# Half-array products strictly in turn, and a new order of the steps of the last two thirds, in a sketched-attention and multiplicative-FFN kernel

## The chip, the cores and the metric

The kernel runs on one core of a Trainium2 chip. The core has five engines with a queue of instructions each: TensorE (PE in the profile, its weight loads as PEld), VectorE (DVE), ScalarE (ACT), GpSimd (POOL) and SyncE (SP), which issues the transfers here. The metric is the device time of one execution in microseconds (us). Each engine runs its own instructions in the order in which the program lists them; engines wait for each other by semaphores.

## The reference

Inputs are float64. First comes attention with a polynomial sketch, for 4 batches, 4 heads, 1088 positions and head size 32, with sketches of 8 rows:

```python
def phi(x):
    a = np.einsum('rd,bhsd->bhsr', S1, x)
    b = np.einsum('rd,bhsd->bhsr', S2, x)
    return np.einsum('bhsi,bhsj->bhsij', a, b).reshape(*x.shape[:-1], r * r)
q_p, k_p = (phi(q), phi(k))
kv = np.einsum('bhsf,bhsd->bhfd', k_p, v)
z = np.sum(k_p, axis=2)
num = np.einsum('bhsf,bhfd->bhsd', q_p, kv)
den = np.einsum('bhsf,bhf->bhs', q_p, z)[..., None] + 1e-06
attn = num / den
```

The result, as x with 4352 rows and 128 columns, goes through a multiplicative FFN with 1024 inner columns; the output is float32:

```python
a = x @ w1
b = x @ w2
h = a * b @ w3
return h @ w_out
```

## The kernel before

**Steps and their order.** `make_steps` defines some 1,100 named steps; each one issues one or a few instructions, or transfers. The text `ORDER` lists all names once, and the last function runs the steps in this order and chains the instructions of each engine, so that ORDER fixes every engine's queue. An engine that waits holds up all that stands behind it in its own queue. Four more tables belong to ORDER: `POOL` names the steps that run on GpSimd instead of VectorE (`on(name)`), `CPV` names copies that run on VectorE instead of ScalarE (`cp(name)`), and `SLOTS` gives for each kind of tile the buffer that every new tile takes, in the order in which ORDER creates them. Kind "b" is the eight PSUM banks. A tile that takes a buffer waits until all who used its former tile are done. The transfers on SP's queue are issued in turn, and each bulk load waits until the fourth bulk transfer before it has landed.

**Weights.** `wN.load`, `.c`, `.m`, `.j`, `.a0`, `.a1` fetch a quarter or an eighth of the float64 weights into one of three buffers (kind "raw") and make float32 of them: c and m on ScalarE read the buffer and so release it, j runs on VectorE, a on GpSimd. w0 and w1 make w1 and w2, w2 makes w_out (`wo`), w3 to w10 the eight row blocks of w3. `fK.t`, `.m`, `.o` fold block K of w3 with w_out into `w3o`: a transposition on VectorE, 8 matmuls, a copy.

**Keys and queries.** The steps `kB.*` make batch B's key sketch, its sum and its product with v (`kv0` to `kv3` and `kvr`, the last for the 64 rest positions, from `vB.load` and `vB.loadr`). `kB.ab` makes the sketch of the keys and `kB.abt` turns it. The steps `qG.*` make x, transposed, for group G of tokens: `tr`, `A0`, `C0`, `C1`, `At`, `Ct`, the arithmetic of the quotient, `phi`, `pT`, then `x` (matmuls into four banks) and `xT` (copies out of them). Group "r" holds the 64 rest positions of all batches. q4 stands for groups 4 and 5, q6 for 6 and 7.

**FFN, groups 0 to 3 and r.** For each of 8 column blocks c, `gG.ca` and `gG.cb` are the products with w1 and w2, `cc` copies the first out of PSUM, `cm` multiplies. `gG.co` accumulates the product with `w3o`, `gG.oT` turns the sum on VectorE, `gG.st` stores it (four transfers). Group r has half the columns, and `gr.co0` and `gr.co1`.

**FFN, groups 4 to 7: the block part.** `seven(g)` computes the products with w1 and w2 for two groups at once with seven products instead of eight, each with 64 rows. Half a (u = 0) holds the chain for w1 and uses array rows 0 to 63, half b (u = 1) the one for w2 and rows 64 to 127, so that a product of a and one of b can run together. For each g (4 or 6), i (0 to 3) and half there are the steps `h{g}.{i}{a or b}{1..7}` (products) and c, d, e, i (copies by ScalarE) and f, g, h (adds by VectorE). In their order: 1 into bank X, copy c; 5 into bank Y, copy d; 6 onto X, copy e; 3 onto Y, add f; 7 onto X, add g; 2 into bank Z, add h; 4 onto X, which half a copies (i). Product 6 waits for copy c, 7 for e, 4 for g, and 3 for d, as the bank is read in between. Then `m11`, `m12`, `m22` multiply halves a and b out of SBUF (VectorE or GpSimd), and `m21` takes half b from the bank (VectorE). `h{g}.s1` to `s4` make the sums of inputs that the products need: 5 needs s1, 6 needs s2, 7 needs s3, 3 needs s4, and s2 reads s1, s4 reads s2. The `v.*` steps make the same for the weights. `g4.co` to `g7.co` are the products with `w3o`, `g.oS` rescales (VectorE or GpSimd).

In ORDER the block part of h4 comes after the output products of groups 0 to 3, then those of g4 and g5, then h6, then those of g6 and g7 mixed with group r. The lines that the change touches are the tables SLOTS, POOL, CPV and ORDER; the lines that the prediction names are 1644 (products of the block part), 1651 (its copies), 1656 (adds), 1678 and 1683 (m), 1519 (x), 1625 (s2), 1697 and 1707 (a and b), 1732 (o), 1721 (o of group r), 1739 (oT), 1745 (oS), 1548 (stores), 432 (weight loads), 967 (q loads), 579 (v loads), 1325 (tr), 719 (ab) and 526 (folds).

Of the kernel before, what the change touches and what calls it, by code (L numbers as in the profile page):

```python
# [43 lines left out]

WARM = [27, 2, 3, 4, 4, 4, 1, 2, 1, 1, 2, 2, 1, 1]
# [49 lines left out]
g2.7c w7.m w7.c k3.kT1 k0.Nr q4.tr g1.1m g1.0m g2.2a q3.al q3.p2 q3.p12 q3.dn q3.de g1.4b g2.4a g2.5a g2.5c w3.load
k3.rest0 w5.j w6.j w6.a0 g1.4m k3.gram0 k3.gram1 k3.gram2 k3.gram3 k3.gram4 k3.Gm k3.Gt q3.rc k3.Ga k3.kT0 q3.bs k3.Gb
g2.3a w5.a1 g2.2c w2.m q2.restT q4.max w7.j g2.1a g2.1c g2.1b g2.1m g2.5b g2.5m g2.7b g1.6b g2.6a k3.Gc g2.3c k2.Nb
q4.l2 q3.load q3.restT qr.max qr.l2 qr.l1 g2.4c w3.m g2.6c g2.0b g2.0a g2.0c w8.load w4.load v3.zero v3.loadr v2.load
v3.load v2.loadr k2.Nr q3.phi0 q3.pT0 g0.2m w7.a1 w2.a0 g1.6m kr1.kp k3.T0 w6.a1 w7.a0 w2.a1 w5.a0 k3.T1 g2.2b g2.6b
g2.4b g2.3b f6.t w3.c k3.Ta g2.7m k3.Tb g2.4m k3.Tc g2.6m f4.t w3.j w3.a1 q3.x f6.m q3.xT0 w3.a0 g3.7a q4.l1 g3.3a v.s  # L100
g3.7c f6.o f4.m f4.o g2.2m q4.A0 g2.0m g3.3c g2.3m q4.rm f3.t k3.ab k3.N0 w10.load q4.C0 q4.C1 k3.N1 k2.kp0 g3.6a
k3.abt k3.kp0 q6.tr w4.m f0.t q4.At k2.kp1 q4.Ct g3.0a f3.m w4.c g3.6c w10.c w10.j g3.7b g3.5a g3.3b f0.m g3.7m q4.sm
k3.kp1 f0.o k2.kv0 k2.kv3 k2.kv1 k2.kv2 k3.kv0 k2.kvr k3.kv1 k3.kv3 k3.kv2 v.t g3.0c k3.kvr k3.Na w4.j w4.a0 w4.a1
f2.t g3.3m q4.st q4.sh k3.Nb f1.t k2.kvc q6.max q6.l2 g3.1a f2.m g1.0o k3.Nr g3.5c k3.kvc g2.0o g3.1c f2.o w8.m q4.sl
q4.sc q4.p01 g3.6b g3.1b f1.m g3.6m q4.al q4.p2 q4.p12 g3.5b f3.o f1.o q6.l1 g3.4a g3.0b k3.kqt g3.4c w10.m g1.1o
g3.1m q4.dn k3.kq q4.de g3.5m k2.kqt g2.4o q6.rm g2.6o q4.rc q4.bs q4.nb q4.na g3.0m q6.A0 q6.C0 q6.C1 w8.c w8.j
w10.a1 w8.a1 w8.a0 q6.Ct w10.a0 g1.6o g3.4b g3.2a k2.kq g3.2b g1.3o q4.nm q6.At f5.t f5.m q6.sm g3.4m q6.st qr.rm
q4.nr q4.ne q6.sh g3.2c qr.A0 qr.C0 qr.C1 qr.At qr.sm q4.nn qr.Ct f5.o g2.5o f7.t q4.phi0 q4.phi1 g1.4o g2.3o g2.2o
# [10 lines left out]
h4.3a5 h4.3a6 h4.3b6 h4.3ae h4.3bh h4.2a3 h4.2b7 h4.3b5 h4.2a4 h4.3be h4.2bg h4.1m22 h4.3ad h4.3bd h4.3a7 h6.s2 h4.2bf
h4.3b7 h4.2b4 h4.3a3 h6.0b1 h4.2ai h4.2af h4.2m22 h4.3ag h4.3af h4.3b3 h4.3a2 h4.3a4 h4.3bg h4.2m21 h4.3ah h4.3bf  # L120
h4.3m12 h4.2m12 h4.3m22 h4.3m11 h6.1a1 h6.1b1 h6.0a5 h4.3b4 h4.3ai gr.1b h4.3m21 gr.0a g5.0o g5.4o g5.1o g5.5o g5.2o
gr.0c g4.0o g4.4o g4.1o g4.5o g4.2o gr.1a g5.6o g5.3o g5.7o h6.1bc h6.0bc h6.1ac gr.1c h6.0ad gr.1m h6.s3 g4.6o g4.3o
g4.7o g4.oT g5.oT h6.1a6 h6.1ae h6.1b5 h6.1b6 h6.0b2 h6.1a5 h6.1ad h6.1be h6.1bd h6.0bh q6.ns h6.1a7 h6.0b6 h6.0a1
h6.s4 h6.1ag h6.0ac h6.1a3 h6.1b3 g5.oS h6.1bf h6.0a6 h6.1af h6.1a4 h6.1b7 h6.0ae h6.0be h6.1bg h6.1b2 h6.1bh h6.0b5
h6.0a3 h6.1ai h6.0bd h6.0a7 h6.0b7 h6.0ag h6.3a1 h6.2a1 h6.1b4 h6.2ac h6.3ac h6.0af h6.0bg h6.0a4 h6.0b3 h6.2b1
h6.1m21 h6.3a2 h6.3b1 h6.2a6 h6.0b4 h6.0ai h6.0bf h6.0m22 g4.oS h6.3ah h6.1a2 h6.2b2 h6.0m21 h6.2bc h6.0m12 h6.1ah
h6.2bh h6.3bc h6.2ae h6.2a7 h6.2a2 h6.2b6 h6.2b5 h6.2a5 h6.3b6 h6.2ah h6.2be h6.3b5 h6.3a6 h6.1m11 h6.2bd h6.2b7
h6.3a5 h6.2ad h6.1m12 h6.2ag h6.2a4 h6.3be h6.3b7 h6.2b3 h6.3bd h6.2a3 h6.3ae h6.2bg h6.2m22 h6.2ai h6.0a2 h6.3a7
h6.2b4 h6.2af h6.3bg h6.1m22 h6.3ad h6.3b2 h6.3b3 h6.3ag h6.3a3 h6.3a4 h6.3b4 h6.0ah h6.3bf h6.2m11 h6.2bf h6.3af
gr.2a h6.3ai gr.2c h6.0m11 gr.6a g7.0o gr.6c g7.4o h6.2m21 gr.3a h6.3bh h6.3m12 g7.1o gr.0b g7.5o g7.2o gr.5a g7.6o  # L130
g6.0o g6.4o h6.3m11 h6.3m22 h6.3m21 h6.2m12 g7.3o g7.7o g7.oT g7.oS g6.1o g6.5o g6.2o g6.6o g6.3o g6.7o g5.st g4.st
gr.3b gr.4a g7.st gr.6b g6.oT gr.3c gr.6m gr.3m gr.2b g6.oS gr.5b gr.4b g6.st gr.5c gr.7b gr.0m gr.5m gr.7a gr.0o1
gr.0o0 gr.6o0 gr.4c gr.7c gr.5o0 gr.1o0 gr.7m gr.4m gr.6o1 gr.5o1 gr.1o1 gr.4o1 gr.3o1 gr.4o0 gr.3o0 gr.2m gr.2o1
gr.7o1 gr.2o0 gr.7o0 gr.oT0 gr.oT1 gr.st1
# [1697 lines left out]
```

## Time and profile before

| | us |
|---|---|
| median of 3 runs | 250.71 |
| lowest and highest run | 250.65, 251.58 |
| the profiled execution | 251.4 |
| its span, first to last instruction | 249.5 |

The mean granted TensorE clock of the profiled execution is 0.998 of full speed. The profile gives each engine's busy time, a strip of 40 slices in which a digit is the busy share in tenths, and the chain of waits: the work that ended last, followed backwards to what released it. A row of a timeline has the start, the time to the end of the last of its instructions, the engine, the line of the kernel, the operation, the tile written and the tiles read, the shape and the count; in brackets the engine's idle time ahead of it and what ended it. The ends of TensorE's instructions are modelled, so the distance of two starts says more than the length of one. A row of a table by stretches has the stretch, its length, then busy time and count of PE, PEld, DVE, ACT and POOL (of PE and PEld alone where only one line's instructions are asked for), the granted clock, the share of time in which the DMA engines were busy, and GB/s. A row of a group has its count, its busy time and the mean in ns of one, and the idle time before. The rows themselves stand with the prediction.

### The profile page before, as it was taken

What the parts mean: (1) busy time and instruction counts of PE and PEld (TensorE: products, weight loads), DVE (VectorE), ACT (ScalarE), POOL (GpSimd) and SP (SyncE); (2) the same over time, 40 slices, a digit from 0 to 9 for tenths busy, and PEclk for the clock granted to TensorE, in tenths of its full rate; (3) what the DMA queues carried; (4) which work ended last, traced back from release to release, by engine and by line L of the source; (5) the groups of instructions that cost most, each with busy time, mean ns of one, the idle gap of its engine ahead of it and who ended that gap; (6) DMA issues with size and microseconds to landing.
All of it is one profiled execution on the core that took longest, in us unless ns stands there. A gap on an engine that the chain in (4) does not pass through costs nothing.

```text
span 249.5 us, 6587 instructions
## 1 busy us (share of the span) xinstructions
PE 242.9 (97%) x2678; PEld 142.5 (57%) x2678; DVE 181.1 (73%) x383; ACT 121.3 (49%) x242; POOL 140.6 (56%) x191
## 2 busy tenths in 40 slices
PE   8999998999999999999999999999999999999994
PEld 5887554654554576864565444554654455755474
DVE  2888889987799897987788989838650258775151
ACT  3878686528887565567002203865530156531010
POOL 4476675509669986773636889571898031380100
PEclk9999999999999999999999999999999999999999
DMA  7676859984879966000000000630000022000022
GB/s 204 180 201 219 215 160 238 218 226 119 221 171 239 226 155 161 3 3 1 3 0 3 1 0 13 105 57 0 0 0 0 0 44 43 0 0 3 10 43 53
DMA packets 31934, 22.06 MB, mean 88 GB/s; under 512 B 21280, under 2 KB 26528, under 8 KB 31904
## 3 DMA queue, kind: packets, MB, share of 16 engines
q1 hardware_dynamic: 31360, 21.11, 34.7%
q10 hardware_dynamic: 544, 0.52, 0.6%
q8 instruction: 21, 0.34, 0.6%
q14 instruction: 9, 0.07, 0.1%
HBM read 19.40 MB, written 2.23 MB: 87 GB/s over the span
## 4 chain that ended last, share of the span: by engine, by line
PE 87%; DVE 5%; DMA 4%; POOL 1%; ACT 1%; SPq 1%; issue 1%; DVEq 0%; ACTq 0%
PE ps_o L1732 22%; PE ps_X L1644 11%; PE b_ps L1707 11%; PE a_ps L1697 10%; PE ps_Y L1644 6%; PE ps_w3o L526 6%; PE idle_ps L247 4%; DMA raw<-in_moe_w_dram 4%; PE ps_Z L1644 3%; PE ps_g L651 2%; PE ps_x L1519 2%; PE ps_ac L1366 2%; PE ps_kv L761 2%; PE ps_or L1721 1%; POOL kk L643 1%; PE ps_kt L677 1%
## 5 line engine op out<-in xcount | busy, mean ns | idle before, releaser
L1644 PE MATMUL ps_X<-xd,wv 64*128 64x512 f32 x112 | 41.0, 601 | 0.1
L1702 ACT COPY ffa<-a_ps 128x512 f32<-128x512 f32 (+1 forms) x38 | 20.1, 541 | 41.4 <-PE a_ps L1697 41.1
L1697 PE MATMUL a_ps<-xT,w 128*128 128x512 f32 (+1 forms) x80 | 36.4, 561 | 0.0
L1707 PE MATMUL b_ps<-xT,w 128*128 128x512 f32 (+1 forms) x80 | 35.9, 557 | 0.1
L1713 DVE TENSOR_TENSOR ab<-ffa,b_ps 128x512 f32<-128x512 f32 (+1 forms) x40 | 24.0, 623 | 14.0 <-ACT ffa L1702 10.6
L1678 POOL TENSOR_TENSOR hc<-hc 128x512 f32<-128x512 f32 x17 | 21.6, 1294 | 21.7 <-DVE hc L1656 21.7
L1651 ACT COPY hc<-ps_X 128x512 f32<-128x512 f32 x40 | 22.3, 595 | 21.3 <-PE ps_X L1644 19.0
L1732 PE MATMUL ps_o<-ab,w3o 128*128 128x512 f32 x64 | 29.1, 597 | 0.0
L1732 PE MATMUL ps_o<-hc,w3o 128*128 128x512 f32 x64 | 28.4, 592 | 0.0
L493 POOL TENSOR_TENSOR w3c<-w3c,cv_m 128x512 int32<-128x512 int32 x16 | 20.1, 1275 | 5.0 <-DVE w3c L487 5.0
L1644 PEld LDWEIGHTS ps_X<-xd,wv 64*128 64x128 f32 x112 | 16.9, 186 | 10.4 <-issue 4.9
L1697 PEld LDWEIGHTS a_ps<-xT,w 128*128 128x128 f32 x80 | 14.4, 189 | 14.3 <-issue 9.0
L1707 PEld LDWEIGHTS b_ps<-xT,w 128*128 128x128 f32 x80 | 14.3, 190 | 13.8 <-issue 9.6
L1644 PE MATMUL ps_Y<-xd,wv 64*128 64x512 f32 x48 | 22.1, 603 | 0.0
L1732 PEld LDWEIGHTS ps_o<-hc,w3o 128*128 128x128 f32 x64 | 12.2, 190 | 12.7 <-issue 12.4
L1732 PEld LDWEIGHTS ps_o<-ab,w3o 128*128 128x128 f32 x64 | 11.6, 190 | 12.9 <-issue 12.8
L526 PEld LDWEIGHTS ps_w3o<-wo,w3T 128*128 128x128 f32 x128 | 15.5, 192 | 3.5 <-issue 3.3
L526 PE MATMUL ps_w3o<-wo,w3T 128*128 128x128 f32 x128 | 15.7, 276 | 0.0
L1739 DVE STREAM_TRANSPOSE oT<-ps_o 128x512 f32<-128x512 f32 x8 | 5.4, 700 | 13.9 <-PE ps_o L1732 9.3
L1532 ACT COPY xd<-ps_x 64x256 f32<-64x256 f32 x16 | 5.9, 366 | 18.0 <-PE ps_x L1519 17.8
L255 ACT ACTIVATE cv_c<-raw 128x1024 f32<-128x1024 f32 (+1 forms) x13 | 13.2, 1019 | 2.7 <-DMA raw<-in_moe_w_dram 2.4
L1656 DVE TENSOR_TENSOR hc<-hc,ps_Z 128x512 f32<-128x512 f32 x16 | 10.8, 683 | 4.8 <-PE ps_X L1644 2.9
(315 smaller groups left out, 514.5 us busy)
## 6 DMA issues: line engine op xcount, KB each, us to landing
raw<-in_moe_w_dram SPq DMA_DIRECT2D x32, 256.0 KB, 4.7
qh<-in_q_dram SPq DMA_DIRECT2D x4, 544.0 KB, 3.8
raw<-in_moe_w_dram SPq DMA_DIRECT2D x4, 512.0 KB, 6.8
out_dram<-oT SPq DMA_DIRECT2D x32, 64.0 KB, 1.9
k<-in_k_dram SPq DMA_DIRECT2D x3, 512.0 KB, 4.3
v<-in_v_dram SPq DMA_DIRECT2D x2, 512.0 KB, 5.1
kh<-in_k_dram SPq DMA_DIRECT2D x8, 128.0 KB, 3.1
raw<-in_moe_w_out_dram SPq DMA_DIRECT2D x4, 256.0 KB, 5.4
```

The lines of the kernel that those rows point to most:

```text
L255: act.activation(dst, hi.bitcast(F32), ACT.Prelu, scale=2.0 ** -112, alpha=-2.0 ** 32)
L493: pool.tensor_tensor(d, d, x["m"][:, i * 512:(i + 1) * 512], ALU.add)
L526: pe.matmul(t["o"], w3T[ko][:, c], wo[:, c], start=c == 0, stop=c == NC - 1)
L1644: pe.matmul(x[bank], stat(j, u)[:, i * 128:(i + 1) * 128], rows(j, u), start=new, stop=True, tile_position=(u * 64, 0), skip_group_check=True)
L1651: act.copy(x[k], x[bank])
L1656: dve.tensor_add(x[k], x[k], x[bank])
L1678: on(f"h{g}.{i}m{k}").tensor_mul(both[0][k], both[0][k], both[1][k])
L1697: pe.matmul(x["a"][:, :w], w_of(0, c), xT[g][:, c0:c0 + w], start=True, stop=True)
L1702: cp(f"g{g}.{c}{su}c")(x["s"][:, :w], x["a"][:, :w])
L1707: pe.matmul(x["b"][:, :w], w_of(1, c), xT[g][:, c0:c0 + w], start=True, stop=True)
L1713: dve.tensor_mul(ab_sb[g, c][:, c0:c0 + w], x["s"][:, :w], x["b"][:, :w])
L1732: pe.matmul(o_ps[g], w3o[:, c], ab_sb[g, c], start=c == turn[0], stop=c == turn[-1])
```

## The change

The first 313 names of ORDER stay as they were, up to the step g1.7a. From there on the steps stand in a new order. In the block part the products of half a and half b alternate, except at one place; before, 40 products followed one of their own half. SLOTS has new buffers for the tiles from there on. Some steps change engine: of the m products eight of h4 and four of h6 leave GpSimd for VectorE and two of h6 go the other way, as do some small steps of q4, q6 and qr; the copies g2.1c, g2.5c, g2.6c, g3.4c, gr.1c, gr.4c, k2.kq and k3.kq go from ScalarE to VectorE (the names k3.kT0 and k3.kT1 in CPV change nothing, since those steps do not use `cp`). What is computed does not change. The diff, cut to what is spoken of:

```diff
 POOL = set("""
-    g4.oS g5.oS g7.oS h4.0m11 h4.0m12 h4.0m22 h4.1m11 h4.1m12 h4.1m22 h4.2m12 h4.2m22 h4.3m11 h4.3m12
-    h4.3m22 h4.s1 h4.s2 h4.s4 h6.0m11 h6.0m12 h6.1m12 h6.1m22 h6.2m11 h6.2m22 h6.s1 h6.s2 h6.s4 k0.Nf
+    g4.oS g5.oS g6.oS h4.0m11 h4.0m12 h4.2m22 h4.s1 h4.s3 h4.s4 h6.0m22 h6.1m12 h6.1m22 h6.3m22 h6.s1
+    h6.s3 h6.s4 k0.Nf k0.Nh k0.Nr k0.kp1 k1.Nr k1.kp1 k2.Nr k2.kp0 k2.kp1 k2.rest0 k3.Nr k3.kp0 k3.kp1
...
 CPV = set("""
-    g0.1c g0.3c k0.kT1 k1.kvc k2.kT1 q0.xc0 q0.xc1
+    g0.1c g0.3c g2.1c g2.5c g2.6c g3.4c gr.1c gr.4c k0.kT1 k1.kvc k2.kT1 k2.kq k3.kT0 k3.kT1 k3.kq
+    q0.xc0 q0.xc1
...
 ORDER = """
...
-k1.kqt warm12 w6.c w6.m g0.3b k1.kq g1.5c g1.4a k3.max g1.4c w5.load g1.1b kh3.load q2.load g1.3m g1.5m g1.2m g1.0c
-q2.pT0 warm13 g1.0b k2.Tc q2.x g0.3m w9.a1 w5.m q2.xT0 k2.N0 k2.N1 w5.c g0.2b w9.a0 k2.Na w7.load k3.lead0 w2.j g2.7a
+g1.3b k1.kqt warm12 w6.c w6.m g0.3b k1.kq g1.5c g1.4a k3.max g1.4c w5.load g1.1b v2.loadr kh3.load k0.Nr q2.load g1.3m
+g1.5m g1.2m g1.0c q2.pT0 warm13 g1.0b k2.Tc q2.x g0.3m w9.a1 w5.m q2.xT0 k3.kT0 k2.N0 k2.N1 w5.c q3.al q3.p2 q3.p12
+q3.dn w6.j g1.0m q3.de w7.load w2.m g1.4b w7.m w7.c w3.load w10.load w4.load v2.load w2.j k2.Na g1.4m k2.Nb q3.rc
...
+w3.a0 g3.1c g2.0m k2.kp1 q6.tr k3.Tc g2.7m w7.a1 f4.t g3.6a q3.restT g3.6c q4.A0 w3.a1 q6.max k3.ab
...
-h4.0b1 h4.0a2 h4.0ac q6.xT3 h4.0ah q6.xT0 h4.0b5 h4.0a6 h4.0ae h4.1b5 h4.0a5 h4.0a7 q6.xT1 qr.rc h4.s4 h4.0bc h4.2b1
-h4.0ad h4.0bd h4.1bd h4.0b6 h4.0a3 h4.1a1 qr.bs h4.0ag h4.0bh qr.phi0 h4.0b3 qr.pT0 h4.0a4 h4.0be h4.1ac h4.0b7 h4.0ai
-h4.2bc h4.1b3 h4.1a6 h4.0bf h4.0af g1.st g2.st h4.0bg qr.x qr.xT0 h4.1ae h4.0m22 h6.s1 h4.0b4 h4.2a1 h4.1b1 h4.0m21
+g2.2o qr.rc qr.bs qr.phi0 q6.pT0 g1.oT g2.1o g2.7o q6.pT1 g3.7o qr.pT0 h4.s1 g2.oT g3.oT qr.x v.2 qr.xT0 q6.x h4.0a1
+h4.s2 h4.0b1 h4.1a1 q6.xT0 q6.xT1 h4.0b5 h4.0ac h4.0bc g3.st g2.st g0.st g1.st h4.0a6 h4.0b2 h4.0a5 h4.0bd h4.0ae
...
+g5.6o h4.3m11 h4.3m12 gr.0a gr.0c h6.0ad h6.1bc gr.1c h6.0bc g5.3o g5.7o g4.6o gr.1b g5.oT gr.1m g4.3o g4.7o gr.0b
+g4.oT h6.s2 h6.1b2 h6.s3 gr.0m h6.s4 h6.1bh h6.1a2 h6.1ac h6.0b2 h6.1a6 h6.1b5 h6.1ae h6.0bh h6.0a1 h6.1ah h6.1b6
...
+g6.1o g6.5o g6.2o g7.1o g7.5o g6.6o gr.4a g7.2o g7.6o g7.3o g7.7o gr.6a g6.3o gr.5a g6.7o g6.oT g6.oS gr.4c gr.5c
+gr.3a gr.6c gr.6m g5.st g4.st g6.st gr.5m g7.oT gr.7c gr.0o0 gr.2b gr.2a gr.4b gr.6o0 gr.5o0 gr.3b gr.0o1 gr.6o1 gr.7b
```

More of the change, by code (lines that the diff above doesn't have):

```diff
@@ L94 @@
-q2.pT0 warm13 g1.0b k2.Tc q2.x g0.3m w9.a1 w5.m q2.xT0 k2.N0 k2.N1 w5.c g0.2b w9.a0 k2.Na w7.load k3.lead0 w2.j g2.7a
[L95 to L108, printed above, removed]
@@ L119 @@
[L119 to L133, printed above, removed]
@@ L134 @@
-gr.7o1 gr.2o0 gr.7o0 gr.oT0 gr.oT1 gr.st1
+k3.load g1.7a v.s g1.7b g1.2a v1.load g1.7c q2.sl q2.sc q2.p01 q2.al q2.p2 k2.Gc q3.At g0.0b k1.kp1 q3.sm q3.st k1.kv0
+q3.sh k2.T0 k1.kv2 k1.kv3 k1.kv1 k2.T1 k1.kvr k1.kvc kr1.kp g1.2c k2.Ta q2.p12 q2.dn q2.de k2.Tb g0.0m q2.rc g0.6m
+q3.sl q3.sc q3.p01 w9.j g1.7m q1.restT q2.bs g1.6a g1.6c w2.c v2.zero q2.phi0 g1.2b k3.loadr g1.3a g1.3c g1.0a g1.5b
+g1.3b k1.kqt warm12 w6.c w6.m g0.3b k1.kq g1.5c g1.4a k3.max g1.4c w5.load g1.1b v2.loadr kh3.load k0.Nr q2.load g1.3m
@@ new lines @@
+g2.7a g2.3b g1.6m q4.l2 w3.m k3.Gc w7.a0 g2.0b f6.o g2.3m w5.a0 w6.a1 v3.zero g2.1m q3.x q4.l1 k3.T0 k3.T1 g2.6m w3.j
+g2.7c q4.rm g2.5b g2.5m q3.xT0 q3.load g2.7b g3.0a v3.load w8.load v3.loadr k3.Ta w4.m g3.0c g3.0b g3.0m g3.3a g3.1b
+g3.1a g3.3c k3.Tb w3.a0 g3.1c g2.0m k2.kp1 q6.tr k3.Tc g2.7m w7.a1 f4.t g3.6a q3.restT g3.6c q4.A0 w3.a1 q6.max k3.ab
+k3.N0 k3.abt k2.kp0 q4.C0 q4.C1 k3.N1 f4.m k3.kp1 g3.6b f0.t f3.t f4.o k3.kp0 f0.m q4.At q6.l2 g3.6m k2.kv0 k2.kv3
+g3.1m w4.c w4.j k3.kv0 k3.kv1 k3.kv3 k3.kv2 k3.kvr q4.Ct q4.sm q6.l1 qr.max k3.kvc k2.kv1 k2.kv2 k2.kvr k2.kvc f3.m
@@ L135 @@
+gr.7o0 gr.oT0 gr.oT1 gr.st1
 """
```

64 lines of the change are left out of this document (40 added, 24 removed).

## The prediction

> **What bounds the kernel now.** I read the page's totals, slices and chain of waits first, then the tables of busy time by stage, and last the timeline inside the block part.
>
> ```profile
> span 249.5 us, 6587 instructions
> PE 242.9 (97%) x2678; PEld 142.5 (57%) x2678; DVE 181.1 (73%) x383; ACT 121.3 (49%) x242; POOL 140.6 (56%) x191
> ...
> PE   8999998999999999999999999999999999999994
> ...
> PE 87%; DVE 5%; DMA 4%; POOL 1%; ACT 1%; SPq 1%; issue 1%; DVEq 0%; ACTq 0%
> ```
>
> TensorE sets the end: 87% of the chain is its own, and from the second slice on it hardly shows a hole. The matrix products are the same before and after, so an order can win only where TensorE works below its pace, and lose wherever it makes TensorE wait. So I looked for lost pace. Outside the block part I found little after 64 us: products of the same form follow each other at 0.43 us a pass (each float32 product is two passes). The block part is different. Its products use 64 rows of the array, so two run side by side. The table of busy time for the block products alone, in their three runs:
>
> ```profile
> 153.77:162.70 8.93, 8.93 (x36) 4.63 (x36) 1.00 0.53 90
> 163.58:183.56 19.98, 19.91 (x84) 11.49 (x84) 1.00 0.05 9
> 198.87:222.68 23.81, 23.81 (x104) 14.00 (x104) 1.00 0.13 23
> ```
>
> These are 224 passes in 52.72 us. "Busy" counts a single half as busy, so it hides the loss. The timeline has the pace:
>
> ```profile
> 207.50 0.59 PE L1644 MATMUL ps_X<-xd,w 64*128 64x512 f32 x1
> 207.87 0.59 PE L1644 MATMUL ps_X<-xd,wv 64*128 64x512 f32 x1
> 207.93 0.59 PE L1644 MATMUL ps_X<-xd,w 64*128 64x512 f32 x1
> 208.36 0.59 PE L1644 MATMUL ps_X<-xd,w 64*128 64x512 f32 x1
> ```
>
> The rows with `w` are half a: 207.50, 207.93 and 208.36, 0.43 us apart; the one with `wv` is half b, running beside it. Perfect pairing therefore takes 112 x 0.43 = 48.2 us, and **4.6 us are lost**. That is the ceiling of what the block part can give.
>
> Who takes the 4.6 us? The order there reads h6.3a1 h6.2a1 h6.1b4: two a's in a row, then a b. By the rows, 3a1 runs 207.50 and 207.93, 2a1 begins at 208.36, yet 1b4, behind it in the order, begins at 207.87. A product whose half is taken does not hold up the other half. So neighbours of the same half cost nothing here; the loss is something else:
>
> ```profile
> 172.67 0.69 DVE L1656 TENSOR_TENSOR hc<-hc,ps_Z 128x512 f32<-128x512 f32 x1 [0.58 <-PE ps_X L1644]
> 172.86 0.59 PE L1644 MATMUL ps_X<-xd,w 64*128 64x512 f32 x1
> 173.28 0.68 DVE L1656 TENSOR_TENSOR hc<-hc,ps_Y 128x512 f32<-128x512 f32 x1
> 174.01 0.18 PEld L1644 LDWEIGHTS ps_Y<-xd,wv 64*128 64x128 f32 x1 [0.30 <-DVE hc L1656]
> 203.47 0.29 PEld L1644 LDWEIGHTS ps_Y<-xd,w 64*128 64x128 f32 x2 [0.62 <-ACT hc L1651]
> ```
>
> Half a was free at 173.29 (its last pass began at 172.86) and started at 174.01, when a VectorE add had emptied its bank: 0.7 us lost. At 203.47 a product of half b waits for a ScalarE copy. **The loss is waits for the engines that empty PSUM**, not pairing.
>
> **The change, part by part.** The sum is made against the profiled execution, 251.4 us (span 249.5 and 1.9 around it), 0.7 above the median 250.71 of the runs; the difference is then carried to the median.
>
> *Strict turn in the block part.* Adjacent products of one half fall from 40 to 1. By the rows at 207.50 that alone is worth nothing. What matters is how far a bank's next product stands behind the one whose result must first be copied or added (1 to 6, 6 to 7, 7 to 4, 5 to 3 of one i and half). Counted along each half's own row of products in ORDER, 13 such pairs stand at distance two before, 7 after. Distance two leaves one product, 0.86 us, for a 0.6 or 0.68 us copy or add and its signals; distance three leaves 1.7. If the 4.6 us are shared out over the close pairs, each costs 0.35, and six fewer bring **-2.1 us**. Bounds: all waits gone is -4.6, all kept elsewhere 0, and a slower block is possible (below).
>
> *qr.x leaves the block part* and stands ahead of it.
>
> ```profile
> 162.79 0.85 PE L1519 MATMUL ps_x<-pT,kq 32*32 32x64 f32 x64
> 163.58 0.69 PE L1644 MATMUL ps_X<-xd,wv 64*128 64x512 f32 x1
> 163.97 0.69 PE L1644 MATMUL ps_X<-xd,w 64*128 64x512 f32 x1
> ```
>
> Its own 0.8 us stays. Gone is half a's late start, 0.39 us behind the other while the bank of qr.x is copied out (0.2 on the mean of the halves), and one restart, about 0.1: **-0.3**. Bounds 0 and -0.4.
>
> *New waits at the two starts.* q6.x now follows qr.x, and its banks need g3.oT, 0.70 us on VectorE after the last product of g3, against 0.8 us of qr.x; with some 0.2 us before VectorE begins and 0.1 after: **+0.2** (0 to 0.5). At the second start h6.s2 stands behind g4.oT, which needs the last product of g4; before, s2 was done long ahead. 0.2 + 0.70 + 0.68 (by the L1678 row of VectorE, the same shape) and a signal make 1.7 us, against 0.43 for gr.0b and 0.86 for the first pair: **+0.3** for h6.1a6 (0 to 0.5; s4 behind it, 1.3 on POOL by the nearest row, L1678, is due two pairs later). The rows are among these groups:
>
> ```profile
> L1656 DVE TENSOR_TENSOR hc<-hc,ps_X 128x512 f32<-128x512 f32 x16 | 10.9, 684 | 4.4 <-PE ps_X L1644 2.8 <-ACT hc L1651 1.6
> L1678 POOL TENSOR_TENSOR hc<-hc 128x512 f32<-128x512 f32 x17 | 21.6, 1294 | 21.7 <-DVE hc L1656 21.7
> L1678 DVE TENSOR_TENSOR hc<-hc 128x512 f32<-128x512 f32 x7 | 4.6, 685 | 0.0
> L1739 DVE STREAM_TRANSPOSE oT<-ps_o 128x512 f32<-128x512 f32 x8 | 5.4, 700 | 13.9 <-PE ps_o L1732 9.3 <-DMA out_dram<-oT 4.4
> L1745 POOL TENSOR_TENSOR oT<-oT,nz 128x512 f32<-128x512 f32 x3 | 3.1, 1047 | 17.7 <-DVE oT L1739 17.7
> L1424 DVE TENSOR_TENSOR s_pr<-s_hl 128x128 f32<-128x128 f32 x1 | 1.3, 1326 | 0.0
> ```
>
> *Ten more of the L1678 products go from POOL to VectorE* (eight in h4, two in h6). VectorE starts one every 0.6 us (172.67 to 173.28), so h4 gets about 4.8 us more. In its two runs VectorE has this much room:
>
> ```profile
> 153.77:162.70 8.93, 8.93 (x41) 4.63 (x36) 8.05 (x17) 7.86 (x18) 5.71 (x6) 1.00 0.53 90
> 163.58:183.56 19.98, 19.91 (x90) 11.49 (x84) 13.69 (x22) 10.24 (x22) 13.85 (x26) 1.00 0.05 9
> ```
>
> The third engine column is VectorE: 21.7 of 28.9 us, so 7.2 idle. The products fit, and those placed last are needed only by the output products of g5 and g4, half a dozen us later; but the cover is thin. A product set in front of an add delays a bank by 0.6 us. Taken at **+0.1**; with no cover it is +4.8. By the Trainium skill (SBUF — State Buffer, Who interferes with whom) a VectorE instruction with two SBUF inputs and a GpSimd one that reads SBUF shut each other out for a whole instruction. The L1424 row agrees: 1326 ns for 128 columns, where 512-column products take 685. At 1.3 us for each of ten products that would be up to +13 us of VectorE time.
>
> *The middle, 67 to 152 us.* Moves of g2, g3, folds and q steps change no TensorE work; four 512-column copies and k3.rest0 come to VectorE, q4 and q6 steps go both ways. On the queues, w10.load, w4.load and v2.load now stand ahead of q3.load:
>
> ```profile
> 68.16 2.90 SPq L432 DMA_DIRECT2D raw<-in_moe_w_dram  x4
> 73.88 0.35 SPq L967 DMA_DIRECT2D qh<-in_q_dram  x1
> 74.73 8.57 SPq L432 DMA_DIRECT2D raw<-in_moe_w_dram  x8
> 84.04 6.92 SPq L579 DMA_DIRECT2D v<-in_v_dram  x8
> 90.26 1.95 PE L526 MATMUL ps_w3o<-wo,w3T 128*128 128x128 f32 x16
> 92.26 0.61 PE L719 MATMUL ps_ab<-kT,KS 64*32 64x256 f32 x16
> 93.69 1.20 DVE L1325 STREAM_TRANSPOSE qT<-qh 128x1024 f32<-128x1024 f32 x1
> ```
>
> ```profile
> qh<-in_q_dram SPq DMA_DIRECT2D x4, 544.0 KB, 3.8
> ```
>
> Three 1 MB weight loads and q3.load (3.5 MB) took 68.16 to 84.04. With the three alone ahead, v2.load begins near 68.2 + 15.9 x 3.0/3.5 = 81.8; half of 6.9 us for it puts q3.load at 85.3 and its landing at 89.1. VectorE's q6.tr (1.20) waits for it; queued behind are g2.7m (0.6), which frees a bank, and k3.abt. TensorE's k3.ab (92.26 before) gets five a/b products more ahead of it (4.3 us) and one such and one fold less (0.9 and 1.8), so it is due near 93.9, and q3.load may land as late as 91.9. Margin 2.8 us: **0**, up to +3. v2.loadr, now ahead of kh3.load, holds that up some 2 us, and k3.kT0 needs it only at 65: 0.
>
> *The tail.* g7.st is now issued behind g6.st.
>
> ```profile
> 154.39 9.49 SPq L1548 DMA_DIRECT2D out_dram<-oT  x16
> 242.22 3.73 PE L1721 MATMUL ps_or<-w3o,ab 128*128 128x128 f32 x32
> ```
>
> A store is four issues, 2.4 us. From the last g6 product: 0.2 + 0.7 (transpose) + 1.05 on POOL, then two stores, 6.8 us. TensorE has six 256-column products (half of 0.86 each, 2.6) and the 32 passes (3.7) left, then a copy of some 0.3: 6.6. So gr.st1 comes some 0.2 late: **+0.1** (0 to 1).
>
> Sum: -2.1 - 0.3 + 0.2 + 0.3 + 0.1 + 0 + 0.1 = **-1.7**: 249.7 in a profiled execution like this one, **249.0 us** in the runs.
>
> **The rivals.**
> A, in-order halves: a product whose half is taken holds up the next. Walking ORDER so gives 63 slots before, 56 after: 7 x 0.86 = 6.0 us. More than the 4.6 lost, and the rows at 207.87 speak against it; capped at 4.6, with 0.7 of costs, 246.8. By the Trainium skill (TensorE: Matmul & The Clock Gate, The mechanism) matmuls start strictly in program order, which is this rival, uncapped 244.7; the trace disagrees, 208.36 against 207.87. Chance 0.13.
> B, the waits only change place: VectorE, at 75% in h4 and given 4.8 us more, becomes what the banks wait for, and nothing of the 4.6 is won. For: every quoted wait ended at an emptying engine. Against: 13 close pairs become 7. 250.7 + 0.5 = 251.2, between 250.2 and 252. Chance 0.20.
> C, slower: q3.load lands late. For: the loads ahead of it wait for ScalarE to release their buffers. Against: 2.8 us of margin. Each us beyond 91.9 is a us of TensorE; it decides over the block's gain from 1.7 us beyond, a landing after 93.6; at 7 us later than worked out, 249.0 + 4.2 = 253.2. Chance 0.14.
>
> **How the numbers follow.** My forecast has 0.53, between 247.9 and 250.3 alone. 0.5% is 1.25 us, about what a measurement of this kernel tells from no change: faster is below 249.5, slower above 252.0. Faster: three quarters of the forecast and A, 0.53. Same: the rest of the forecast and most of B, 0.28. Slower: C and the upper end of B, 0.19. The range 246.6 to 251.6 takes in A and most of B; C is left out.
>
> **What would show it.** Right: the three runs become two, about 50 us for 224 passes, with second-half starts still led by waits for hc. A right: 48.2. B: 52 us or more, and VectorE near full there. At the second start h6.1a6 waits for xd from VectorE. C: TensorE idle near 94 us behind VectorE's 128x1024 transpose, which waits for a DMA. Wrong altogether if TensorE shows holds of several us between 67 and 152, or if the store at the end is released by another store.

## The result and the profile after

Beside the kernel before on the same chip, the changed kernel took 250.44 us in the median against 252.17 us. The ratio is **0.9929**, 95% interval 0.9901 to 0.9957: 0.7% faster, or 1.8 us on the 250.7 us of before. The forecast was 249.0 against 250.71, a ratio of 0.993.

The page of the changed kernel, head, slices and chain:

```profile
span 250.6 us, 6584 instructions
PE 241.0 (96%) x2678; PEld 143.0 (57%) x2678; DVE 192.1 (77%) x402; ACT 117.5 (47%) x234; POOL 124.5 (50%) x180
...
PE   8978999999999999999999999999999999999994
...
PE 78%; DVE 11%; DMA 4%; issue 2%; SPq 2%; ACT 1%; POOL 1%; DVEq 0%; ACTq 0%
```

The span of this one execution is longer than before (249.5), although the median is lower. The third and fourth slices say why: they hold a hole that was not there (7 and 8 tenths busy, 9 and 9 before). The table of waits of TensorE in the first 30 us has

```profile
PE ps_krt L811 <- DMA kr<-in_k_dram: 2.1, 1, 2.1
```

and the last of the warm-up products, the one fixed mark ahead of all that the change moves, starts late by 2.96 us (before, then after):

```profile
64.17 0.27 PE L247 MATMUL idle_ps<-zeros 128*128 128x256 bf16 x1
```

```profile
67.13 0.27 PE L247 MATMUL idle_ps<-zeros 128*128 128x256 bf16 x1
```

The names of ORDER are the same up to beyond this transfer, so this is one execution's start and not the change. The late keys are only part of the 2.96: the first product behind the wait starts 2.0 us later than before (19.64 against 17.63), and the lag then grows to 3.5 us (24.31 against 20.84), while the granted clock is 0.66; in the same stretch of before it was 1.00. Table of busy time, after:

```profile
20.00:25.00 5.00, 5.00 (x162) 4.73 (x162) 2.77 (x7) 3.13 (x8) 3.11 (x4) 0.66 0.22 64
```

From here on only stretches behind this mark are compared. The table of busy time after, for the block products alone and then with all engines:

```profile
158.51:185.54 27.03, 26.70 (x120) 15.04 (x120) 1.00 0.23 37
201.28:224.12 22.84, 22.84 (x104) 15.02 (x104) 1.00 0.14 24
```

```profile
158.51:185.54 27.03, 26.70 (x125) 15.04 (x120) 22.78 (x39) 17.86 (x36) 13.64 (x26) 1.00 0.23 37
201.28:224.12 22.84, 22.84 (x105) 15.02 (x104) 16.95 (x28) 12.34 (x23) 11.37 (x24) 1.00 0.14 24
```

Two runs instead of three, 224 passes in 49.87 us, where perfect pairing takes 48.2: of the 4.6 us that were lost, 1.7 are left. VectorE rose to 22.78 of 27.03 us in the first run; the experiment on the m products below finds no cost in that.

With the starts of the rows shown, the whole difference adds up (after less before, us):

| stretch | before | after | difference |
|---|---|---|---|
| start of the span to the last warm-up product | 64.17 | 67.13 | +2.96 (one execution) |
| from there to the last four passes of groups 0 to 3 | 86.37 | 87.32 | +0.95 |
| from there to the first block product (after: with qr.x) | 3.23 | 4.06 | +0.83 |
| block part of h4 (before: with qr.x) | 29.79 | 27.03 | -2.76 |
| between the block parts | 15.31 | 15.74 | +0.43 |
| block part of h6 | 23.81 | 22.84 | -0.97 |
| from there to the end of the span | 26.82 | 26.48 | -0.34 |

Without the first line the sum is -1.86 us, and the runs show -1.8. The last four passes stand at 150.54 before and 154.45 after. The +0.43 and -0.34 go together: by ORDER, gr.0b moved from the tail to the place between the block parts.

The block part gained 2.85 us net of qr.x (52.72 to 49.87), and the middle, where nothing was forecast, lost 0.95. The timeline of after has two holds of TensorE there:

```profile
75.19 1.45 PE L1697 MATMUL a_ps<-xT,w 128*128 128x512 f32 x3
...
73.10 2.58 POOL L1501 TENSOR_TENSOR ph<-s_al,s_bs 128x1024 f32<-128x1024 f32 x1
73.94 2.29 DVE L487 TENSOR_SCALAR w3c<-cv_c 128x1024 int32<-128x1024 int32 x1
76.14 1.27 DVE L1713 TENSOR_TENSOR ab<-ffa,b_ps 128x512 f32<-128x512 f32 x2
76.88 1.12 PE L1707 MATMUL b_ps<-xT,w 128*128 128x512 f32 x2 [0.23 <-DVE ab L1713]
...
80.49 1.23 DVE L1325 STREAM_TRANSPOSE qT<-qh 128x1024 f32<-128x1024 f32 x1
81.65 1.20 DVE L520 STREAM_TRANSPOSE w3T<-w3c 128x1024 f32<-128x1024 f32 x1
82.13 0.27 PE L651 MATMUL ps_g<-k,kk 128*32 128x32 f32 x4
83.00 0.80 PE L526 MATMUL ps_w3o<-wo,w3T 128*128 128x128 f32 x5 [0.60 <-DVE w3T L520]
```

At 76.88 a product waits for a bank that the multiplication g1.1m (76.14) empties; that one stands behind w5.j on VectorE (73.94), which took 2.29 us. The last of the three passes ahead of it (75.19, 0.43 apart) started at 76.05, so 0.83 us passed where 0.43 is the rule: 0.40 lost. At 83.00 the fold f6.m waits for its transposition f6.t (81.65), which stands behind q4.tr (80.49): some 0.8 us lost. Together the two are 1.2 us, a little more than the 0.95.

### The profile page after: what moved, and what is told of

Its sections match the earlier page's. It is cut to its first block, busy times and chain, and to the rows that moved or that the text cites. A ratio compares the mean times of both kernels' runs of the same rounds, so it can differ in the third digit from the quotient of the medians.

```text
span 250.6 us, 6584 instructions
## 1 busy us (share of the span) xinstructions
PE 241.0 (96%) x2678; PEld 143.0 (57%) x2678; DVE 192.1 (77%) x402; ACT 117.5 (47%) x234; POOL 124.5 (50%) x180
## 4 chain that ended last, share of the span: by engine, by line
PE 78%; DVE 11%; DMA 4%; issue 2%; SPq 2%; ACT 1%; POOL 1%; DVEq 0%; ACTq 0%
PE ps_o L1732 22%; PE ps_X L1644 11%; PE a_ps L1697 9%; PE b_ps L1707 8%; PE ps_w3o L526 6%; PE ps_Y L1644 6%; PE ps_Z L1644 3%; DMA kr<-in_k_dram 2%; PE ps_ac L1366 2%; DVE ab L1713 2%; PE ps_kv L761 2%; PE ps_x L1519 2%; DMA k<-in_k_dram 2%; PE ps_g L651 1%; PE ps_or L1721 1%
## 5 line engine op out<-in xcount | busy, mean ns | idle before, releaser
L1644 PE MATMUL ps_X<-xd,wv 64*128 64x512 f32 x112 | 43.0, 596 | 0.3 <-issue 0.3
L1707 PE MATMUL b_ps<-xT,w 128*128 128x512 f32 (+1 forms) x80 | 36.9, 560 | 0.3 <-DVE ab L1713 0.2
L1702 ACT COPY ffa<-a_ps 128x512 f32<-128x512 f32 (+1 forms) x32 | 16.9, 547 | 41.4 <-PE a_ps L1697 41.3
L1732 PE MATMUL ps_o<-hc,w3o 128*128 128x512 f32 x64 | 29.3, 595 | 0.0
L493 POOL TENSOR_TENSOR w3c<-w3c,cv_m 128x512 int32<-128x512 int32 x16 | 21.0, 1326 | 6.3 <-DVE w3c L487 6.3
L1644 PEld LDWEIGHTS ps_X<-xd,wv 64*128 64x128 f32 x112 | 18.8, 186 | 8.6 <-issue 3.4
L1644 PE MATMUL ps_Y<-xd,wv 64*128 64x512 f32 x48 | 23.2, 595 | 0.0
L1678 POOL TENSOR_TENSOR hc<-hc 128x512 f32<-128x512 f32 x7 | 8.8, 1275 | 13.3 <-DVE hc L1656 11.8
L530 ACT COPY w3o<-ps_w3o 128x128 f32<-128x128 f32 x8 | 2.1, 272 | 26.2 <-PE ps_w3o L526 26.2
L1656 DVE TENSOR_TENSOR hc<-hc,ps_Y 128x512 f32<-128x512 f32 x16 | 10.7, 682 | 4.0 <-ACT hc L1651 2.8
```

What stands on the lines that cost most here:

```text
L493: pool.tensor_tensor(d, d, x["m"][:, i * 512:(i + 1) * 512], ALU.add)
L1644: pe.matmul(x[bank], stat(j, u)[:, i * 128:(i + 1) * 128], rows(j, u), start=new, stop=True, tile_position=(u * 64, 0), skip_group_check=True)
L1656: dve.tensor_add(x[k], x[k], x[bank])
L1678: on(f"h{g}.{i}m{k}").tensor_mul(both[0][k], both[0][k], both[1][k])
L1702: cp(f"g{g}.{c}{su}c")(x["s"][:, :w], x["a"][:, :w])
L1707: pe.matmul(x["b"][:, :w], w_of(1, c), xT[g][:, c0:c0 + w], start=True, stop=True)
```

## The experiments

Three questions: does the strict turn itself gain, or the greater distances; does the move to VectorE cost; and is the middle's loss what the two rows say. In the numbers of the block part, qr.x (0.85 us, 0.98 in the last of the four kernels that follow one rule) is taken off where it lies inside. Times and ratios come from several runs of each kernel, but the figures of stretches come from one profiled execution of each. Two kernels with the same block part, the changed one and the one with two moves in the middle, took 49.87 and 49.85 us for it. The rows of patterns and the four kernels that follow one rule were run once each.

**Turn alone, and rows alone.** First the kernel before with a and b strictly in turn, each half's own row as before (here and in the next two, the first twelve products of ORDER, without the steps between them):

```diff
-h4.0a1 h4.0b2 h4.0b1 h4.0a2 h4.0b5 h4.0a6 h4.1b5 h4.0a5 h4.0a7 h4.2b1 h4.0b6 h4.0a3
+h4.0a1 h4.0b2 h4.0a2 h4.0b1 h4.0a6 h4.0b5 h4.0a5 h4.1b5 h4.0a7 h4.2b1 h4.0a3 h4.0b6
```

> The kernel before, with the products of half a and half b strictly in turn; each half keeps its own row of products, every other engine its own order, every tile its buffer. The 13 close pairs at distance two stay, the products that follow one of their own half go from 40 to none. Theory of the prediction (waits for the engines that empty PSUM): the block part stays at 52.7 us for its 224 passes, within 0.7, and the time stays that of the kernel before, within 0.5%. Rival A (a product whose half is taken holds up the next): by the walk through ORDER, 62 slots of 0.86 become 56, so the block part falls by 4 to 5 us, to 48 to 49, and the time by 1.6% or more. If strict turn alone gives what the whole change gave, the block part comes out at 49.9.

The time was 250.97 against 252.13, ratio 0.9968 (0.9927 to 1.0008), which alone does not tell it from no change. Twelve close pairs remain rather than thirteen, since h6's first products, which stand among those of h4, changed places too. Walked in strict order, ORDER gives 63 slots before, as the prediction has it, and 57 here; the difference of six is the expectation's. Its table:

```profile
155.61:185.05 29.44, 27.98 (x120) 13.29 (x120) 1.00 0.21 37
200.37:223.44 23.07, 23.07 (x104) 13.59 (x104) 1.00 0.14 23
```

That is 52.51, less 0.85 for qr.x 51.66: in the trace the turn alone gains 1.1 us. That is more than the 0.7 of the prediction's theory, and far from 4 to 5.

Second, the changed kernel's rows with the old pattern, all other engines as in the changed kernel:

```diff
-h4.0a1 h4.0b1 h4.1a1 h4.0b5 h4.0a6 h4.0b2 h4.0a5 h4.0b6 h4.0a7 h4.1b5 h4.0a2 h4.0b3
+h4.0a1 h4.0b1 h4.0b5 h4.1a1 h4.0b2 h4.0a6 h4.0b6 h4.0a5 h4.0a7 h4.1b5 h4.0b3 h4.0a2
```

> The changed kernel with the pattern of a and b that stood before (40 products follow one of their own half); each half keeps the changed kernel's own row of products. Theory of the prediction: the block part stays at 49.9 us, within 0.7, and the time stays that of the changed kernel, 0.993 of before. Rival A: 56 slots become 62, the block part goes to about 55 us and the time to 2% over the changed kernel.

The time was 254.32 against 252.13, ratio 1.009 (1.0055 to 1.0125), and the block part took 54.43:

```profile
156.80:185.70 28.90, 28.61 (x120) 15.06 (x120) 1.00 0.21 35
201.44:226.97 25.53, 24.77 (x104) 13.71 (x104) 1.00 0.12 21
```

The theory of the prediction missed by 4.6 us, and rival A was near. The new rows without the turn, with copies and adds in the order made for the turn, are slower than the old ones.

| block part, us | old pattern | strict turn |
|---|---|---|
| old rows | 52.7 (before) | 51.7 |
| new rows | 54.4 | 49.9 (after) |

**Runs of three**, where rival A should be plainest:

```diff
-h4.0a1 h4.0b1 h4.1a1 h4.0b5 h4.0a6 h4.0b2 h4.0a5 h4.0b6 h4.0a7 h4.1b5 h4.0a2 h4.0b3
+h4.0a1 h4.0b1 h4.1a1 h4.0a6 h4.0a5 h4.0b5 h4.0b2 h4.0b6 h4.0a7 h4.0a2 h4.0a3 h4.1b5
```

> The changed kernel with the products in runs of three, a a a b b b, in most of both block stretches; each half keeps its own row. Theory of the prediction, if a free half may start past a product that waits for the other: the block part stays near 49.9 us, at most 1 us more for the few starts at which one half has nothing to do. Rival A, in order: 56 slots become 74, 18 x 0.86 = 15.5 us more, block part 65, time 6% over before.

The time was 267.19 against 252.13, ratio 1.0632 (1.0576 to 1.0687), the block part 67.2 us (33.43 and 33.73). That is rival A's number, and 2 us more. But the number is not the mechanism, as the next one shows.

**The same patterns where nothing waits for another engine.**

```diff
+    for zi, pat in enumerate(("ab" * 12, "aabb" * 6, "aaabbb" * 4, "aaaabbbb" * 3)):
+        @step(f"z{zi}")
...
+            for u in pat:
+                p = slice(0, 64) if u == "a" else slice(64, 128)
+                pe.matmul(t[u], w12[p, 1, 0, :128], w12[p, 0, 0], start=True, stop=True,
+                          tile_position=(0 if u == "a" else 64, 0), skip_group_check=True)
...
+            if n == 4:
+                act.copy(sb("hc", [128, 512], name="hc"), t["a"])
```

> The changed kernel with four rows of 24 products of 64 array rows behind its end, 12 of half a and 12 of half b, which wait for no other engine: a b in turn, in twos, in threes and in fours; each row begins with one product of the whole array. A fifth row has nine: a b a b, a ScalarE copy out of a's bank, then a (which must wait for that copy) and four of b. In perfect pairs a row takes 12 x 0.86 = 10.3 us. Theory of the prediction (neighbours of one half cost nothing): 10.3 us for all four. Rival A (strictly in order): 10.3, 11.2, 14.6 and 16.3. Between them, if just one product whose half is taken can be passed: 10.3, 10.3, 11.2 and 12.0. Fifth row: if a product that waits for another engine holds only its own half, the first of the four b begins 1.72 us after the first product; if it holds all behind it, it begins with the waiting a, 0.7 us or more later.

Table of busy time, the four rows in order:

```profile
244.85:255.27 10.42, 10.41 (x48) 4.56 (x48) 1.00 0.05 14
256.41:266.93 10.52, 10.52 (x48) 6.10 (x48) 1.00 0.01 2
268.07:279.44 11.37, 11.37 (x48) 6.76 (x48) 1.00 0.00 0
280.59:293.26 12.67, 12.67 (x48) 6.80 (x48) 1.00 0.00 1
```

The rows stand behind the end of the kernel and change nothing that it computes. They take 10.4, 10.5, 11.4 and 12.7 us: near the numbers of "just one can be passed" (10.3, 10.3, 11.2, 12.0; the fours are 0.7 above), far from those of a strict order (14.6 and 16.3 for the last two). Twos cost 0.1 us in 24 products; threes cost one product at the start of the row and none after. So runs of three cost 1 us where nothing waits and 17 where products wait. And the fifth row shows what a wait does:

```profile
295.80 0.59 PE L1790 MATMUL idle_za<-w 64*128 64x512 f32 x1
295.81 0.59 PE L1790 MATMUL idle_zb<-w 64*128 64x512 f32 x1
296.42 0.59 ACT L1789 COPY hc<-idle_za 128x512 f32<-128x512 f32 x1 [52.06 <-PE idle_za L1790]
297.06 0.69 PE L1790 MATMUL idle_za<-w 64*128 64x512 f32 x1 [0.67 <-ACT hc L1789]
297.07 0.69 PE L1790 MATMUL idle_zb<-w 64*128 64x512 f32 x1
```

Half b was free from 296.24 (295.81 and a pass of 0.43), its next product needed nothing, and it started at 297.07, 0.01 behind the product of half a that waited for the copy. **A product whose half is taken can be passed by one of the other half; a product that waits for another engine is passed by none, and holds both halves.**

The waits in the block part itself bear this out. For each kernel every idle time of a half over 0.05 us (the start of a product less the last pass of its half and 0.43) was set beside the end of the copy or add that the product needs, from the trace. Idle time that its own copy or add ended, and idle time in which the product was ready and stood behind another one, summed over both halves, so that half of it is time of the block part (the starts behind qr.x are left out):

| | own wait, us | held behind another, us |
|---|---|---|
| before | 4.0 | 1.4 |
| turn alone | 1.4 | 1.1 |
| new rows, old pattern | 4.6 | 4.6 |
| after | 1.0 | 0.7 |
| runs of three | 16.2 | 16.8 |

Most of what the turn alone took away is a product's own wait (4.0 to 1.4), and little of it is the holding of another (1.4 to 1.1); by what way the turn shortens these own waits no run shows. The table leaves out what follows a wait: the two passes of the first product behind it stand some 0.53 us apart instead of 0.43 (297.06 and 297.60 behind the wait above). Summed the same way that is 2.9 us before and 1.7 after.

One place of a held product, in the new rows with the old pattern: h6.3b4 waits for an add, and h6.3a2, ready since 223.75, starts with it.

```profile
223.80 0.59 PE L1638 MATMUL ps_Z<-xd,w 64*128 64x512 f32 x1
224.41 1.28 DVE L1650 TENSOR_TENSOR hc<-hc,ps_X 128x512 f32<-128x512 f32 x2 [1.33 <-PE ps_Z L1638]
225.15 0.69 PE L1638 MATMUL ps_X<-xd,wv 64*128 64x512 f32 x1 [0.76 <-DVE hc L1650]
225.15 0.69 PE L1638 MATMUL ps_Z<-xd,wv 64*128 64x512 f32 x1
```

**The same with the emptying engines re-ordered.** In the runs above, copies and adds kept the order made for another pattern. Four more kernels have them in the order of their products by one rule, which gives out the buffers too.

> Control for the next three. The changed kernel with its own products in turn, but the block part's copies, adds and m products ordered by one rule on their engines: each copy and add at one fixed distance behind the product that it reads, each m product behind the last of what it multiplies; buffers given to the one longest unused. Both theories: block part near the changed kernel's 49.9 us, between 49.5 and 51.5.

> The same rule with the pattern of a and b of before (40 products behind one of their own half). Theory 1: with no waits such neighbours cost nothing (rows of fours cost 2 us in 24 products, of twos 0.2), and the 4.6 us that the old pattern cost earlier came from copies and adds left in the order of the strict turn: block part within 1 us of the control. Theory 2: the pattern itself costs, since a product that waits for its bank holds both halves, and out of turn more of them wait: block part 3 to 5 us above the control, as in the earlier run.

> The same rule with runs of three. Theory 1: block part within 2 us of the control (one product of 0.86 at the start of each run of the block, as in the row without waits). Theory 2: the wait behind each product that has to wait is now up to two products longer, and the block part stays over 60 us, as in the earlier run with 67.

> The kernel before, its products in turn, each half with its own old row (twelve pairs at distance two against seven), and the same rule for copies, adds and m products; qr.x stays inside the block part (0.9 us, left out of the numbers). If the close pairs carry the gain, 0.35 us each as predicted: block part 1.5 to 2 us above the control. If the turn carries it: within 0.5 us of the control.

In the one run of each the times were 256.84, 262.03, 266.56 and 260.56 us in this order, against 251.16 for the kernel before. By their tables of busy time the block part took 28.74 + 23.47 = 52.2 us (control), 30.18 + 25.10 = 55.3 (old pattern), 31.21 + 28.57 = 59.8 (threes) and 32.17 + 24.45 less 0.98 = 55.6 (turn with old rows). The control is 2.3 us above the changed kernel, outside what was expected: the rule is a poorer order. Against it the old pattern costs 3.1 us (theory 2) and threes 7.6, neither within the 2 of theory 1 nor over 60. So about 10 of the 17 us of threes (17.3 less 7.6) went with the new order of copies, adds and buffers, and the pattern keeps a cost of its own where products wait. The last one says little on the size of what the rows do. At 183.25 both halves start late, by 2.49 and 1.79 us: one product waits for a bank that a late m product still reads, and the other is held behind it.

```profile
182.51 0.68 DVE L1677 TENSOR_TENSOR hc<-hc,ps_X 128x512 f32<-128x512 f32 x1
183.25 0.69 PE L1638 MATMUL ps_Y<-xd,wv 64*128 64x512 f32 x1 [1.63 <-DVE hc L1677]
183.25 0.69 PE L1638 MATMUL ps_Y<-xd,w 64*128 64x512 f32 x1
```

Half of the two, 2.1 of the 3.4 us above the control, comes from the buffer that the rule gave out and not from the rows. The remaining 1.3 stands beside the 1.8 (51.7 less 49.9) of the table above.

**The m products back on their old engines.**

```diff
 POOL = set("""
-    g4.oS g5.oS g6.oS h4.0m11 h4.0m12 h4.2m22 h4.s1 ... h6.0m22 h6.1m12 h6.1m22 h6.3m22
+    g4.oS g5.oS g6.oS h4.0m11 h4.0m12 h4.0m22 h4.1m11 h4.1m12 h4.1m22 h4.2m12 h4.2m22 h4.3m11
+    h4.3m12 h4.3m22 h4.s1 ... h6.0m11 h6.0m12 h6.1m12 h6.1m22 h6.2m11 h6.2m22
```

> The changed kernel with the m products (line 1678) on the engines of before: twelve go back from VectorE to GpSimd, two from GpSimd to VectorE. Theory of the prediction: VectorE has room for them, so they cost 0.1 us; the block part stays at 49.9, within 0.4, and the time within 0.3% of the changed kernel; the output products behind the block may wait up to 0.5 us for GpSimd, whose products take 1.28 us against 0.69. Rival B (VectorE is the bound in the block part): without the load of twelve products, 8.3 us, the remaining 1.7 us of waits go, and the block part comes to 48.2 to 48.8.

The time was 250.17 against 252.13, ratio 0.9923 (0.9891 to 0.9956), and the block part 50.07 us (27.08 and 22.99). Nothing came back with the load gone from VectorE: rival B falls, and the move cost nothing that can be measured.

**The two holds of the middle.**

```diff
-g2.2a w5.j g1.1m g0.2m q3.phi0
+g2.2a g1.1m g0.2m w5.j q3.phi0
...
-w2.a1 q4.tr k3.gram0 w6.a0 w5.a1 f6.t g2.2m
+w2.a1 k3.gram0 w6.a0 w5.a1 f6.t g2.2m q4.tr
```

> The changed kernel with two steps of VectorE further back: w5.j behind g1.1m and g0.2m, q4.tr behind f6.t and g2.2m. Theory: the two holds of TensorE in the middle, 0.40 us at 76 (a bank waits for g1.1m, behind w5.j) and 0.78 at 82 (f6.m waits for f6.t, behind q4.tr), come from the order of VectorE's queue; without them the time falls by about 1.2 us, to 0.988 of before. Rival: VectorE, 29 of 31 us busy there, is the bound of that stretch, the holds come again a few us later, and the time stays 0.993 of before.

The time was 247.83 against 251.67, ratio **0.9856** (0.9801 to 0.9912): faster than both kernels by its middle value, though its interval overlaps the changed kernel's (0.9901 to 0.9957) at the edge. The trace is sharper. First its timeline, with the last warm-up product and two passes of the middle, then its table of busy time, whose stretch begins with the first block product:

```profile
63.58 0.27 PE L241 MATMUL idle_ps<-zeros 128*128 128x256 bf16 x1
...
72.50 0.59 PE L1691 MATMUL a_ps<-xT,w 128*128 128x512 f32 x1
72.93 0.59 PE L1701 MATMUL b_ps<-xT,w 128*128 128x512 f32 x1
```

```profile
153.82:180.84 27.02, 26.69 (x120) 15.40 (x120) 1.00 0.23 37
```

The two passes at 72.50 and 72.93 are those that stood 0.83 apart, and are 0.43 apart now. From mark to block part it is 153.82 - 63.58 = 90.24 us against 158.51 - 67.13 = 91.38: 1.14 us less, the 1.2 of the two holds, and neither came again. The block part is as it was. The theory holds, and the rival, VectorE as the bound of that stretch, falls.

**The old middle with the new block part.**

> The order and the engines of the kernel before up to the block part (with the last six steps of qr set ahead of it, so that qr.x is outside as in the changed kernel), and of the changed kernel from its first block product on. Theory: the gain comes from the block part alone and the new middle costs about 1 us, so that this kernel is faster than both: block part 49.9 us, the middle as before, time 0.988 to 0.990 of before. Rival: the block part needs the new middle (VectorE or ScalarE come to it with work left), the block part stays above 51 us, and the time is not below the changed kernel's 0.993.

The time was 262.65 against 251.67, ratio 1.041 (1.0367 to 1.0453), and it answers nothing of the question: ahead of the block part qr.bs was set behind six instructions of the v group on GpSimd (1.26 us each), and TensorE waited 6.95 us, up to 160.61. Table of busy time, all engines:

```profile
155.00:160.00 5.00, 0.00 (x0) 0.00 (x0) 0.25 (x1) 0.00 (x0) 4.69 (x6) 0.72 0.00 2
160.00:165.00 5.00, 4.08 (x130) 2.73 (x132) 2.56 (x5) 0.88 (x5) 0.94 (x1) 0.50 0.26 44
165.00:170.00 5.00, 4.44 (x16) 1.58 (x14) 3.31 (x9) 4.57 (x12) 0.00 (x0) 0.76 0.69 118
```

The block part took 52.3 us there, above the 51 of the rival, but it began at 164.62, at a lowered clock. Whether the new block part would pay as much behind the old middle stays open.

## Why the prediction was right, and where it was not

The time came out as forecast, but in part by luck: the middle came out 0.95 us worse than forecast and everything else together 1.1 us better, so that the errors cancelled.

- **Strict turn, -2.1, and qr.x out of the block, -0.3.** Together -2.4; measured -2.85. The size is nearly right, the reason only in part. "Adjacent products of one half ... that alone is worth nothing" is the step that failed: the turn alone gained 1.1 us. The rows at 207.50 showed one product passing another whose half was taken, and that is true (twos cost 0.1 us in 24 products). But the prediction went on as if the halves never held each other up. They do as soon as a product waits for an engine, and the same prediction had named such waits as the whole loss. That holding is the smaller share of the waits before (1.4 of 5.4 us in the table above); why the turn also shortens the products' own waits stays open. Turn and rows work together: 1.1 us by the turn with old rows, a loss of 1.7 by the new rows without the turn, 2.85 with both. The price of 0.35 us for a close pair fits in strict turn, where five pairs fewer go with 1.8 us, and not in the old pattern, where the new rows made it slower. Since copies, adds and buffers changed with the rows, no run shows that the 1.8 comes from the pairs.
- **The cause of the loss, waits for the engines that empty PSUM:** right, as the larger part. They fell from 5.4 us of idle halves to 1.7 in the table above, which is 1.9 us of the block part; the slow first passes behind waits are another 0.6 (2.9 to 1.7 us of idle halves).
- **The starts, +0.2 and +0.3.** The way to the first start is longer by 0.83 us. qr.x starts there at 156.26 and q6.x at 156.84 in the trace, so 0.58 is qr.x itself and 0.25 is left, near the forecast. At the second, h6.1a6 did wait for s2 on VectorE, but briefly:

```profile
201.60 0.65 DVE L1620 TENSOR_TENSOR xd<-xd 128x512 f32<-128x512 f32 x1
...
202.25 0.59 PE L1644 MATMUL ps_Z<-xd,w 64*128 64x512 f32 x1
202.40 0.66 PE L1644 MATMUL ps_X<-xd,wv 64*128 64x512 f32 x1
```

s2 ended at 202.25 and 1a6 started at 202.40, 0.15 us after the other half's pass.
- **Ten m products on VectorE, +0.1:** nothing, by the experiment. The 13 us that products shut out by GpSimd might have cost did not arise: the 17 products of line 1678 that ran on VectorE took 686 ns in the mean, and none of them started behind a running GpSimd instruction. Rival B was given 0.20 and fell.
- **The middle, 0 with up to +3 by one transfer:** +0.95, by something else. q3.load did start later, as worked out, and q6.tr did not wait for it; rival C fell:

```profile
88.89 0.36 SPq L967 DMA_DIRECT2D qh<-in_q_dram  x1
```

```profile
95.14 0.69 DVE L1713 TENSOR_TENSOR ab<-ffa,b_ps 128x512 f32<-128x512 f32 x1
95.74 1.24 DVE L1325 STREAM_TRANSPOSE qT<-qh 128x1024 f32<-128x1024 f32 x1
```

Without the 2.96 us of this execution's start the issue is at 85.93; 85.3 was worked out. VectorE went straight from one step to the next at 95.74. What the prediction did not do is walk VectorE's queue, to which it had itself counted four copies and k3.rest0 as added, against TensorE's next need. Such a walk would have met q4.tr, of 1.23 us, ahead of f6.t. The hold behind w5.j it would hardly have found: the same instruction took 0.69 us at 70.34, with GpSimd idle, and at that length w5.j would have ended near 74.6 and g1.1m near 75.3 (an estimate from these rows), ahead of the 76.48 at which the product was due. It took 2.29 us with a GpSimd instruction at work beside it (last section).
- **The tail, +0.1:** nothing. gr.st1 was not held by the stores of g6 and g7:

```profile
242.83 4.18 SPq L1548 DMA_DIRECT2D out_dram<-oT  x8
247.40 0.62 SPq L1554 DMA_DIRECT2D out_dram<-oT  x1
```

- **Rival A** in its strict form falls by the patterns alone, 11.4 us for threes where 14.6 were due. Its number in two kernels (55 and 65 expected, 54.4 and 67.2 measured) goes with waits that hold both halves and with copies and adds left in another order. A number that fits is not yet a mechanism.

## What to carry to other kernels

Where two streams of work share one in-order queue, count what a waiting item holds of the other stream: here strict turn-taking gained 1.1 us alone, the new rows alone cost 1.7, and both together gained 2.85. Re-order the emptying engines with the products: of what runs of three cost, about 10 of 17 us went with the new order of copies, adds and buffers, and of what the old pattern cost, 1.5 of 4.6. After a wholesale re-ordering, look on the busiest helper engine (VectorE here) for long steps set ahead of short ones that the bottleneck needs: two such steps moved back were worth as much as 40% of the block part's gain, and one of them was long with a GpSimd instruction at work at the same time.

## What the runs showed of the hardware that was not expected

- One product of the free half starts ahead of a product whose half is taken (207.87 against 208.36 us), but no second one (in the row of threes half b starts 0.97 us behind half a), and none past a product that waits for another engine (297.07). So the first section's sentence, that each engine runs its instructions in the listed order, has this exception on TensorE. By the Trainium skill (TensorE: Matmul & The Clock Gate, The mechanism) matmuls start and end strictly in order; with half-array products the patterns alone disagree for threes, 11.4 us against 14.6.
- w5.j, 1024 columns on VectorE (0.69 us for the same instruction at 70.34, with GpSimd idle), took 2.29 us at 73.94 while one GpSimd instruction ran from 73.10 to 75.68, and ended 0.55 us after it; in the kernel with two moves its end (71.56 and 1.11 us) is again 0.55 us behind the end of the GpSimd instruction (69.55 and 2.57; the rows below). A third one, in the changed kernel (119.30 and 1.07 us), ended 0.55 us behind a GpSimd instruction that ended at 119.82.

```profile
69.55 2.57 POOL L1495 TENSOR_TENSOR ph<-s_al,s_bs 128x1024 f32<-128x1024 f32 x1
71.56 1.11 DVE L481 TENSOR_SCALAR w3c<-cv_c 128x1024 int32<-128x1024 int32 x1
```

By the Trainium skill (SBUF — State Buffer, Who interferes with whom) a tensor_scalar of VectorE can run in a 2-port mode, and then it and a GpSimd instruction shut each other out for a whole instruction. The rows agree; which mode it ran in no run shows.
- After 6.95 us without a product (up to 160.61 in the kernel with the old middle) the granted clock of TensorE was 0.50 from 160 to 165 and 0.76 from 165 to 170; a hold of that length costs more than itself. After 2.1 us without one, in the profiled execution of the changed kernel, it was 0.66 from 20 to 25.
- One execution of the same start-up code lost 2.96 us to a transfer of keys that landed late and to the lowered clock behind it, more than the whole change is worth: spans of single executions do not compare kernels, stretches behind a common mark do.
